# Inverse root of the norm: ScalarE's square root, VectorE's reciprocal and a Newton step in place of GpSimd's power

## The chip, the cores and the metric

The kernel runs on one core of one Trainium2 chip. The metric is the device time of one execution in microseconds (us). Five runs of the kernel before gave a median of 1666.22 us, from 1665.01 to 1666.94. Engines are called by the names of the profile: PE (TensorE's matmul), PEld (its weight load), DVE (VectorE), ACT (ScalarE), POOL (GpSimd) and SP (SyncE, which issues DMAs).

## The reference

An attention without softmax, whose output rows are normed per head, feeds a mixture of four experts that are all computed and weighted. Everything is float32.

```python
# q, k, v: (8, 8, 576, 64)
kv = np.einsum('bhsd,bhse->bhde', k, v)
out = np.einsum('bhsd,bhde->bhse', q, kv)
rms = np.sqrt(np.mean(out * out, axis=-1, keepdims=True) + 1e-06)
x = out / rms * g_norm          # then (B,H,S,D) -> (4608, 512)
p = domain_probs / (domain_probs.sum(-1, keepdims=True) + 1e-09)
for e in range(4):              # w1: (4, 512, 1024), w2: (4, 1024, 512)
    h = np.maximum(x @ w1[e], 0.0)
    out += p[:, e:e + 1] * (h @ w2[e])
```

The change concerns the factor 1 / rms: one number for each row and head, 64 elements wide.

## The kernel before, in words

**Work and stages.** The 4608 rows of x are cut into 9 chunks of 512 rows: the first 512 rows of each of 8 batches, and one chunk of the 64 rows that each batch leaves over. The outer loops go over experts and, inside, over chunks (lines 1671 to 1708), so there are 36 steps. A step multiplies by w1 (`up`, or `up_plain` for the first), applies the relu, multiplies by w2 (`down` or `down_deep`), and sends the weighted result to memory. The products are made in fewer multiplications by a two-level scheme of sums and differences of blocks (Strassen's kind). PE does the products (line 410), and DVE, POOL and ACT make the sums (line 433), copy banks of PSUM away (line 1262 and 1576) and merge results (lines 1406 and 1413). Weights and stored forms of x are loaded by SP.

**Attention in between.** The first expert's steps carry the attention of the next batch with them. `opening` does batch 0 ahead of everything, one pair of heads at a time; `attention` does batches 1 to 7, each in two parts of four heads. A part is: k by v (line 1001), a copy of the result (line 1013), q by that (`attend`, lines 1028 and 1037, into two "ab" and two "db" banks), copies of these banks to SBUF (lines 909 and 910, on DVE or ACT), squares (line 927, ACT, back into ab banks), sums over 64 elements (line 933, DVE), the inverse root, the scaling (line 950, DVE), a transposition on PE (`turn_x`, line 1069) and copies with the gain (line 1078, ACT). The left-over rows of both parts are normed together and transposed at line 1090. The opening has the same chain at lines 742 to 814: square 640, sum 647, power 654 and 658, scaling 667, transposition 806, copy 814.

**The norm.** `scaled` (opening, 5 calls) and `norm_rows` (attention, 21 calls) have a function `power` that issues two POOL instructions: a scaling of the sum of squares `ss` by 1/D with the constant added (lines 654 and 940), and ALU power with exponent -0.5 out of the constant tile `mhalf` into `rt` (lines 658 and 944). `ss` and `rt` have two buffers each.

**What sets the order.** Nothing is issued in the order in which it stands in the source. Each piece of work is given to `plan.add` with a key (its place in the steps), a cost for each engine that may do it, and what it reads and writes. `Plan.layout` then plays the program through in planned time: an engine that is free takes, among the operations within reach of its first open key, one whose inputs and buffers are ready, PE and SP the first one, the others the most urgent. Operations with two costs go to whichever of DVE and POOL takes them first. Buffers are assigned on the way. The result is a fixed order of instructions for each engine; on the chip every engine works through its own in that order and waits at each instruction for what it needs. So a changed cost can change every order after it. The costs are measured-looking constants, for instance

```python
def pe(products, columns, passes=2):
    return {"PE": passes * products * (0.0025 + columns / 1200.0) + 0.003}
```

and the constants 1.42 for `key_values` (line 1008) and 1.45 for `attend` (line 1043). `port=True` marks operations that DVE and POOL are kept from doing at the same time. While the first attention's data arrive, the planner fills PE's gaps with transpositions of the identity (line 1712).

Of the kernel before, what the change touches and what calls it, by code (L numbers as in the profile page):

```python
# [10 lines left out]
ACT = mybir.ActivationFunctionType  # L11
ALU = mybir.AluOpType
AX = mybir.AxisListType
ENG = mybir.EngineType
F32 = mybir.dt.float32
# [280 lines left out]
def kernel(  # L296
# [36 lines left out]
    nc = tc.nc  # L333

    B, H, S, D = q.shape
    E, DM, F = moe_w1.shape
    P = nc.NUM_PARTITIONS
# [15 lines left out]
    dram = ctx.enter_context(tc.tile_pool(name="dram", bufs=1, space=bass.MemoryType.DRAM))  # L353

    ident = const.tile([P, P], F32, name="ident")
    mhalf = const.tile([P, 2 * H], F32, name="mhalf")
    gcol = const.tile([P, 1], F32, name="gcol")
    p_all = const.tile([P, NBLK, E], F32, name="p_all")
    tot = const.tile([P, NBLK], F32, name="tot")
# [2 lines left out]
    BANKS = {"u1": 2, "u2": 2, "db": 2, "ab": 2}  # L362
    SHAPE = {
        "big": (31, 2 * NT), "w1y": (7, 768), "xf": (5, 2 * NT), "snap": (5, HN),
        "ss": (2, 2 * H), "rt": (2, 2 * H),
    }
    slots = {
        kind: [
# [32 lines left out]
    plan = Plan()  # L401

    def pe(products, columns, passes=2):
        return {"PE": passes * products * (0.0025 + columns / 1200.0) + 0.003}

    def halves_of(out_, lhsT, rhs, **kw):

# [212 lines left out]
    def x_halves(c):  # L620
        if c not in halves:
            halves[c] = [Buf("big", f"x{c}_{dh}") for dh in range(2)]
        return halves[c]

    def scaled(key, name, raw, n, x, blocks):

        width = blocks * D
        ss, rt = Buf("ss", f"ss{name}"), Buf("rt", f"rt{name}")

        def src(r):
            return raw[r].ap[0:n, 0:width].rearrange("p (b d) -> p b d", d=D)

        for r in range(2):
            plan.add(
                key, act(width),
                lambda eng, r=r: nc.scalar.activation(  # L640
                    out=x.ap[0:n, r * width:(r + 1) * width], in_=raw[r].ap[0:n, 0:width],
                    func=ACT.Square),
                reads=[raw[r]], parts=[x],
            )
        plan.add(
            key, dve(2 * width),
            lambda eng: nc.vector.reduce_sum(
                out=ss.ap[0:n, 0:2 * blocks],
                in_=x.ap[0:n, 0:2 * width].rearrange("p (b d) -> p b d", d=D), axis=AX.X),
            reads=[x], writes=[ss],  # L650
        )

        def power(eng):
            nc.gpsimd.tensor_scalar(
                out=ss.ap[0:n, 0:2 * blocks], in0=ss.ap[0:n, 0:2 * blocks], scalar1=1.0 / D,
                scalar2=EPS, op0=ALU.mult, op1=ALU.add,
            )
            nc.gpsimd.tensor_tensor(
                out=rt.ap[0:n, 0:2 * blocks], in0=ss.ap[0:n, 0:2 * blocks],
                in1=mhalf[0:n, 0:2 * blocks], op=ALU.pow,  # L660
            )

        plan.add(key - 0.3, {"POOL": 0.3 + 0.37 * blocks}, power, reads=[ss], writes=[ss, rt])
        for r in range(2):
            plan.add(
                key, dve(width),
                lambda eng, r=r: nc.vector.tensor_tensor(
                    out=x.ap[0:n, 0:2 * width].rearrange("p (b r d) -> p b r d", r=2, d=D)[:, :, r, :],
                    in0=src(r),
                    in1=rt.ap[0:n, r * blocks:(r + 1) * blocks].unsqueeze(2).to_broadcast(  # L670
                        [n, blocks, D]),
                    op=ALU.mult,
                ),
                reads=[raw[r], rt], **{"parts" if r else "writes": [x]},
            )
# [212 lines left out]
    def attention(b, key, span, rem):  # L888
# [25 lines left out]
        def norm_rows(key, name, x, squares, count):  # L914

            ss, rt = Buf("ss", f"ss{name}"), Buf("rt", f"rt{name}")
            width = count * D

            def by_head(ap):
                return ap.rearrange("p (b d) -> p b d", d=D)  # L920

            for at_ in range(0, width, NT):
                n = min(width, NT)
                sq = squares or Buf("ab", f"sq{name}_{at_}")
                plan.add(
                    key, act(n),
                    lambda eng, sq=sq, at_=at_, n=n: nc.scalar.activation(
                        out=sq.ap[:, 0:n], in_=x.ap[:, at_:at_ + n], func=ACT.Square),
                    reads=[x], writes=[sq],
                )  # L930
                plan.add(
                    key, dve(n),
                    lambda eng, sq=sq, at_=at_, n=n: nc.vector.reduce_sum(
                        out=ss.ap[:, at_ // D:(at_ + n) // D], in_=by_head(sq.ap[:, 0:n]),
                        axis=AX.X),
                    reads=[sq], parts=[ss],
                )

            def power(eng):
                nc.gpsimd.tensor_scalar(  # L940
                    out=ss.ap[:, 0:count], in0=ss.ap[:, 0:count], scalar1=1.0 / D, scalar2=EPS,
                    op0=ALU.mult, op1=ALU.add,
                )
                nc.gpsimd.tensor_tensor(  # L944
                    out=rt.ap[:, 0:count], in0=ss.ap[:, 0:count], in1=mhalf[:, 0:count], op=ALU.pow)

            plan.add(key - 0.3, {"POOL": 0.3 + 0.19 * count}, power, reads=[ss], writes=[ss, rt])
            plan.add(
                key, dve(width),
                lambda eng: nc.vector.tensor_tensor(  # L950
                    out=by_head(x.ap[:, 0:width]), in0=by_head(x.ap[:, 0:width]),
                    in1=rt.ap[:, 0:count].unsqueeze(2).to_broadcast([P, count, D]), op=ALU.mult,
                ),
                reads=[x, rt], writes=[x], port=True,
            )

        xr, xs = Buf("snap", f"x{b}_r"), Buf("snap", f"xs{b}")
        for s in range(2):
# [37 lines left out]
            def key_values(eng, bank=kbank, held=held):  # L996
# [8 lines left out]
                            )  # L1005

            plan.add(
                when, {"PE": 1.42}, key_values, reads=[t for ts in held for t in ts],
                writes=[kbank],
            )  # L1010
            plan.add(
# [9 lines left out]
            def attend(eng, raw=raw, rest=rest, kv=kv, qt=qt, s=s):  # L1021
# [18 lines left out]
                        )  # L1040

            plan.add(
                at(2 * s + 1.0), {"PE": 1.45}, attend, reads=[qt, kv], writes=raw + rest,
                early=True, gang=True,
            )
            when = at(2 * s + 1.4)
# [668 lines left out]

    with tc.manual_schedule(engines={ENG.PE, ENG.DVE, ENG.Activation, ENG.Pool, ENG.SP}):
        make_identity(nc, ident[:])
        nc.vector.memset(mhalf[:], -0.5)
        held = None
        wide = {}  # L1720
        for op in order:
            if op.seed:
                bank, n = op.marks
                assert wide.get((bank.kind, bank.slot), 0) >= n, "a seed would be overwritten"
            elif op.eng == "PE":
                for b in op.outs:
                    wide[b.kind, b.slot] = op.marks[1] if op.marks else 0
            made = op.fn(op.eng)
            if op.port and op.eng == "DVE":
                held = made.ins.name  # L1730
            elif op.port and op.eng == "POOL" and held is not None:
                tc.add_manual_dep(made.ins, held, mybir.DependencyInfo(
                    mybir.DependencyClass.Sync, mybir.DependencyReason.DATA
                ), reason="SBUF port")
# [28 lines left out]
```

## Time and profile before

| | before |
|---|---|
| median of 5 runs | 1666.22 us (1665.01 to 1666.94) |
| the profiled execution's own time | 1666.88 us |
| its span, first to last instruction | 1664.9 us |
| mean granted clock of PE | 0.999 |
| busy: PE, DVE, ACT, POOL | 1652.3, 1249.1, 971.0, 704.6 us |
| chain that ended last: PE's share | 97% |
| power of 16, 8, 4 columns (lines 944, 658) | 3206, 1647, 1140 ns |

The profile is of one execution. Times in it count from the span's start. A group of instructions shows how often it ran, its total, the mean of one, and how long its engine stood idle just before it, with what ended that idle time ("releaser"). PE's busy time holds everything between a matmul's start and its modelled end, so also the time that it takes longer at a lower clock. "PEclk" is the share of full clock that PE was granted. A timeline gives start and duration of merged runs of like instructions, and in brackets the idle time ahead of them.

### The profile page before, as it was taken

What the parts mean: (1) busy time and instruction counts of PE and PEld (TensorE: products, weight loads), DVE (VectorE), ACT (ScalarE), POOL (GpSimd) and SP (SyncE); (2) the same over time, 40 slices, a digit from 0 to 9 for tenths busy, and PEclk for the clock granted to TensorE, in tenths of its full rate; (3) what the DMA queues carried; (4) which work ended last, traced back from release to release, by engine and by line L of the source; (5) the groups of instructions that cost most, each with busy time, mean ns of one, the idle gap of its engine ahead of it and who ended that gap; (6) DMA issues with size and microseconds to landing.
All of it is one profiled execution on the core that took longest, in us unless ns stands there. A gap on an engine that the chain in (4) does not pass through costs nothing.

```text
span 1664.9 us, 66253 instructions
## 1 busy us (share of the span) xinstructions
PE 1652.3 (99%) x28884; PEld 1557.9 (94%) x28884; DVE 1249.1 (75%) x2051; ACT 971.0 (58%) x2391; POOL 704.6 (42%) x701
## 2 busy tenths in 40 slices
PE   9999999999999999999999999999999999999998
PEld 6587888888899999999999999999999999999996
DVE  4768777677788877777778777777788778777774
ACT  3355555554456666666666665656666566666662
POOL 2545453343445343433354554333355455333321
PEclk9999999999999999999999999999999999999999
DMA  9876765535466454444577444444578444444443
GB/s 218 194 228 185 217 176 145 144 126 182 147 168 150 125 122 116 110 114 113 139 182 178 116 117 115 107 113 116 132 178 202 116 116 116 104 115 116 116 104 52
DMA packets 208123, 234.27 MB, mean 141 GB/s; under 512 B 97368, under 2 KB 148440, under 8 KB 207832
## 3 DMA queue, kind: packets, MB, share of 16 engines
q1 hardware_dynamic: 184760, 193.32, 38.6%
q0 software_dynamic: 23072, 36.71, 15.2%
q8 instruction: 227, 3.72, 0.9%
q14 instruction: 64, 0.52, 0.1%
HBM read 155.79 MB, written 74.19 MB: 138 GB/s over the span
## 4 chain that ended last, share of the span: by engine, by line
PE 97%; DVE 1%; DMA 1%; POOL 0%; SPq 0%; issue 0%; ACT 0%; DVEq 0%; POOLq 0%; ACTq 0%
PE u L410 47%; PE db L410 32%; PE ab L410 15%; PE ab L1001 1%; PE ab L1069 1%; PE ab L1028 1%; DMA big<-in_q_dram 0%; DMA big<-in_moe_w_dram 0%; DVE big L433 0%; SPq L439 0%; POOL rt L944 0%; PE ab L1712 0%; PE ab L1090 0%; PE db L1037 0%; DVE small L950 0%
## 5 line engine op out<-in xcount | busy, mean ns | idle before, releaser
L433 DVE TENSOR_TENSOR big<-big,big 128x1024 f32<-128x1024 f32 (+1 forms) x527 | 518.6, 1001 | 39.6 <-ACT big L1226 15.9
L410 PE MATMUL u<-xf,big 128*64 128x128 f32 x6784 | 486.9, 273 | 0.2
L410 PEld LDWEIGHTS u<-xf,big 128*64 128x64 f32 x6784 | 394.0, 137 | 5.4 <-issue 1.0
L410 PE MATMUL u<-xf,w1y 128*64 128x128 f32 x5304 | 385.8, 273 | 0.0
L410 PE MATMUL db<-big,big 128*64 128x128 f32 (+1 forms) x4280 | 361.2, 308 | 2.1 <-DVE snap L909 1.1
L1270 DVE TENSOR_TENSOR big<-u,snap 128x256 f32<-128x256 f32 x476 | 199.5, 421 | 209.3 <-PE u L410 136.3
L433 POOL TENSOR_TENSOR big<-big,big 128x256 f32<-128x256 f32 (+1 forms) x196 | 218.9, 1134 | 226.0 <-DVE big L433 116.7
L410 PEld LDWEIGHTS u<-xf,w1y 128*64 128x64 f32 x5304 | 308.9, 137 | 2.4 <-issue 1.0
L410 PEld LDWEIGHTS db<-big,big 128*64 128x64 f32 x4280 | 262.3, 137 | 43.6 <-issue 2.8
L1262 ACT ACTIVATE snap<-u 128x256 f32<-128x256 f32 x490 | 187.5, 383 | 195.7 <-PE u L410 142.5
L1262 ACT ACTIVATE big<-u 128x256 f32<-128x256 f32 x476 | 181.0, 383 | 66.6 <-PE u L410 41.4
L1576 ACT ACTIVATE snap<-db 128x256 f32<-128x256 f32 (+1 forms) x230 | 82.0, 357 | 116.9 <-PE db L410 106.6
L1226 ACT ACTIVATE big<-big 128x1024 f32<-128x1024 f32 x134 | 140.7, 1050 | 5.6 <-DVE big L433 3.7
L433 POOL TENSOR_TENSOR big<-big 128x512 f32<-128x512 f32 (+1 forms) x76 | 94.3, 1247 | 114.9 <-DVE big L433 82.1
L410 PE MATMUL db<-small,big 128*64 128x128 f32 (+1 forms) x1552 | 116.9, 274 | 0.0
L1429 POOL DMA_DIRECT2D out_dram<-big x108 | 94.3, 1003 | 50.2 <-ACT big L1406 48.0
L1584 DVE TENSOR_TENSOR big<-ab,snap 128x256 f32<-128x256 f32 x166 | 69.9, 421 | 56.2 <-ACT snap L1576 30.1
L1262 ACT ACTIVATE u<-u 128x256 f32<-128x256 f32 x245 | 91.2, 372 | 24.8 <-PE u L410 9.1
L433 DVE TENSOR_TENSOR big<-big 128x512 f32<-128x512 f32 (+1 forms) x131 | 101.0, 783 | 1.0 <-PE u L410 1.0
L1614 POOL TENSOR_TENSOR big<-big 128x512 f32<-128x512 f32 x21 | 26.7, 1274 | 173.6 <-DVE big L433 140.9
L1406 ACT ACTIVATE big<-big,p_all 128x256 f32<-128x256 f32 x200 | 94.5, 501 | 5.4 <-POOL big L1614 4.0
L410 PEld LDWEIGHTS db<-small,big 128*64 128x64 f32 x1552 | 91.3, 137 | 0.7
(193 smaller groups left out, 2336.6 us busy)
## 6 DMA issues: line engine op xcount, KB each, us to landing
xf<-x SPq DMA_DIRECT2D x108, 512.0 KB, 3.6
out_dram<-big POOLq DMA_DIRECT2D x92, 256.0 KB, 5.5
xf<-x_h SPq DMA_DIRECT2D x81, 256.0 KB, 3.3
xf<-x SPq DMA_DIRECT2D x81, 256.0 KB, 3.6
x<-xf SPq DMA_DIRECT2D x36, 512.0 KB, 4.2
big<-in_moe_w_dram SPq DMA_DIRECT2D x32, 512.0 KB, 5.0
x_h<-big SPq DMA_DIRECT2D x18, 512.0 KB, 3.6
out_dram<-big SPq DMA_DIRECT2D x32, 256.0 KB, 3.7
```

The lines of the kernel that those rows point to most:

```text
L410: nc.tensor.matmul(out_[cols], lhsT=lhsT[:, cols], rhs=rhs, **kw)
L433: lambda eng: adder(eng).tensor_tensor(out=out_(), in0=a(), in1=b(), op=op),
L1001: nc.tensor.matmul(bank.ap[r * D:(r + 1) * D, o * D:(o + 1) * D], lhsT=ks[r], rhs=vs[r], start=(j == 0), stop=(j == len(sets) - 1), skip_g ...
L1028: nc.tensor.matmul(raw[r].ap[c * D:(c + 1) * D, (o * NR + t) * D:(o * NR + t + 1) * D], lhsT=qt.ap[half, col:col + D], rhs=kv.ap[half, o * ...
L1226: lambda eng: nc.scalar.activation(out=b.ap[:], in_=b.ap[:], func=ACT.Relu),
L1262: lambda eng: nc.scalar.activation(out=where(), in_=ps.ap[:, 0:HN], func=ACT.Copy),
L1270: lambda eng: nc.vector.tensor_tensor(out=block(whole, a, t), in0=src.ap[:, 0:HN], in1=add_.ap[:], op=ALU.add),
L1406: lambda eng: nc.scalar.activation(out=cell(i, half), in_=ap(), func=ACT.Copy, scale=prob()),
L1429: nc.gpsimd.dma_start(out=dst, in_=cell(i)[parts, :], accum_op=ALU.add)
L1576: lambda eng: nc.scalar.activation(out=where(), in_=group_of(ps.ap), func=ACT.Copy),
L1584: lambda eng: nc.vector.tensor_tensor(out=cell(tq, dq), in0=group_of(src.ap), in1=group_of(add_.ap), op=ALU.add,),
L1614: lambda eng: adder(eng).tensor_tensor(out=whole(to), in0=whole(a), in1=whole(b), op=ALU.add),
```

## The change

The function `power` goes in both places, and with it the tile `mhalf`. A new function `inverse_root` adds two operations to the plan: `root` on ACT, which writes sqrt(ss/D + eps) into `rt`, and `invert` on DVE, four instructions: the reciprocal of `rt` in place, and one Newton step for the inverse root in three instructions that multiply with a scalar and a tensor, with a second part of `rt` (now twice as wide) as scratch. `eps` is a column of constants for ACT's bias. Three costs of the planner change as well: each PE product loses its 3 ns, `key_values` goes from 1.42 to 1.2, and `attend` of batches 1 to 7 from 1.45 to 1.33. Other planner rules are untouched.

```diff
--- before.py
+++ after.py
@@ -353,7 +353,7 @@
     dram = ctx.enter_context(tc.tile_pool(name="dram", bufs=1, space=bass.MemoryType.DRAM))
 
     ident = const.tile([P, P], F32, name="ident")
-    mhalf = const.tile([P, 2 * H], F32, name="mhalf")
+    eps = const.tile([P, 1], F32, name="eps")
     gcol = const.tile([P, 1], F32, name="gcol")
     p_all = const.tile([P, NBLK, E], F32, name="p_all")
     tot = const.tile([P, NBLK], F32, name="tot")
@@ -362,7 +362,7 @@
     BANKS = {"u1": 2, "u2": 2, "db": 2, "ab": 2}
     SHAPE = {
         "big": (31, 2 * NT), "w1y": (7, 768), "xf": (5, 2 * NT), "snap": (5, HN),
-        "ss": (2, 2 * H), "rt": (2, 2 * H),
+        "ss": (2, 2 * H), "rt": (2, 4 * H),
     }
     slots = {
         kind: [
@@ -401,7 +401,7 @@
     plan = Plan()
 
     def pe(products, columns, passes=2):
-        return {"PE": passes * products * (0.0025 + columns / 1200.0) + 0.003}
+        return {"PE": passes * products * (0.0025 + columns / 1200.0)}
 
     def halves_of(out_, lhsT, rhs, **kw):
 
@@ -622,6 +622,27 @@
             halves[c] = [Buf("big", f"x{c}_{dh}") for dh in range(2)]
         return halves[c]
 
+    def inverse_root(key, ss, rt, n, count):
+
+        def root(eng):
+            nc.scalar.activation(
+                out=rt.ap[0:n, 0:count], in_=ss.ap[0:n, 0:count], func=ACT.Sqrt, scale=1.0 / D,
+                bias=eps[0:n, :],
+            )
+
+        def invert(eng):
+            a, r, w = ss.ap[0:n, 0:count], rt.ap[0:n, 0:count], rt.ap[0:n, 2 * H:2 * H + count]
+            nc.vector.reciprocal(out=r, in_=r)
+            nc.vector.scalar_tensor_tensor(
+                out=w, in0=a, scalar=D * EPS, in1=r, op0=ALU.add, op1=ALU.mult)
+            nc.vector.scalar_tensor_tensor(
+                out=w, in0=w, scalar=-0.5 / D, in1=r, op0=ALU.mult, op1=ALU.mult)
+            return nc.vector.scalar_tensor_tensor(
+                out=r, in0=w, scalar=1.5, in1=r, op0=ALU.add, op1=ALU.mult)
+
+        plan.add(key - 0.3, {"ACT": 0.2}, root, reads=[ss], writes=[rt])
+        plan.add(key - 0.3, {"DVE": 0.75}, invert, reads=[ss, rt], writes=[ss, rt], port=True)
+
     def scaled(key, name, raw, n, x, blocks):
 
 
@@ -650,17 +671,7 @@
             reads=[x], writes=[ss],
         )
 
-        def power(eng):
-            nc.gpsimd.tensor_scalar(
-                out=ss.ap[0:n, 0:2 * blocks], in0=ss.ap[0:n, 0:2 * blocks], scalar1=1.0 / D,
-                scalar2=EPS, op0=ALU.mult, op1=ALU.add,
-            )
-            nc.gpsimd.tensor_tensor(
-                out=rt.ap[0:n, 0:2 * blocks], in0=ss.ap[0:n, 0:2 * blocks],
-                in1=mhalf[0:n, 0:2 * blocks], op=ALU.pow,
-            )
-
-        plan.add(key - 0.3, {"POOL": 0.3 + 0.37 * blocks}, power, reads=[ss], writes=[ss, rt])
+        inverse_root(key, ss, rt, n, 2 * blocks)
         for r in range(2):
             plan.add(
                 key, dve(width),
@@ -936,15 +947,7 @@
                     reads=[sq], parts=[ss],
                 )
 
-            def power(eng):
-                nc.gpsimd.tensor_scalar(
-                    out=ss.ap[:, 0:count], in0=ss.ap[:, 0:count], scalar1=1.0 / D, scalar2=EPS,
-                    op0=ALU.mult, op1=ALU.add,
-                )
-                nc.gpsimd.tensor_tensor(
-                    out=rt.ap[:, 0:count], in0=ss.ap[:, 0:count], in1=mhalf[:, 0:count], op=ALU.pow)
-
-            plan.add(key - 0.3, {"POOL": 0.3 + 0.19 * count}, power, reads=[ss], writes=[ss, rt])
+            inverse_root(key, ss, rt, P, count)
             plan.add(
                 key, dve(width),
                 lambda eng: nc.vector.tensor_tensor(
@@ -1005,7 +1008,7 @@
                             )
 
             plan.add(
-                when, {"PE": 1.42}, key_values, reads=[t for ts in held for t in ts],
+                when, {"PE": 1.2}, key_values, reads=[t for ts in held for t in ts],
                 writes=[kbank],
             )
             plan.add(
@@ -1040,7 +1043,7 @@
                         )
 
             plan.add(
-                at(2 * s + 1.0), {"PE": 1.45}, attend, reads=[qt, kv], writes=raw + rest,
+                at(2 * s + 1.0), {"PE": 1.33}, attend, reads=[qt, kv], writes=raw + rest,
                 early=True, gang=True,
             )
             when = at(2 * s + 1.4)
@@ -1715,7 +1718,7 @@
 
     with tc.manual_schedule(engines={ENG.PE, ENG.DVE, ENG.Activation, ENG.Pool, ENG.SP}):
         make_identity(nc, ident[:])
-        nc.vector.memset(mhalf[:], -0.5)
+        nc.vector.memset(eps[:], EPS)
         held = None
         wide = {}
         for op in order:
```

## The prediction

> **What bounds the kernel now.** I read the page first (busy shares, chain), then the waits of PE, then the stretch in which PE waits, by timeline and by windows.
>
> ```profile
> span 1664.9 us, 66253 instructions
> ...
> PE 1652.3 (99%) x28884; PEld 1557.9 (94%) x28884; DVE 1249.1 (75%) x2051; ACT 971.0 (58%) x2391; POOL 704.6 (42%) x701
> ...
> PE 97%; DVE 1%; DMA 1%; POOL 0%; SPq 0%; issue 0%; ACT 0%; DVEq 0%; POOLq 0%; ACTq 0%
> ```
>
> PE is busy for all but 12.6 us. Taking 71 us of work off POOL can't by itself move the end; only a change in what PE waits for can. These are the waits (total, times, longest, us):
>
> ```profile
> PE ab L1069 <- DVE ss L933: 2.5, 1, 2.5
> PE ab L1712 <- POOL ident masks.py:199: 1.4, 1, 1.4
> PE db L410 <- DVE snap L909: 1.1, 1, 1.1
> PE ab L1069 <- DVE small L950: 0.8, 1, 0.8
> ```
>
> The second is the start. The others lie behind a norm. The timeline (start, duration) has the chain of the first two:
>
> ```profile
> 55.78 2.36 POOL L433 TENSOR_TENSOR big<-big,big 128x1024 f32<-128x1024 f32 x1 [10.29 <-DMA big<-in_moe_w_dram]
> ...
> 58.22 1.06 POOL L940 TENSOR_SCALAR ss<-ss 128x16 f32<-128x16 f32 x1
> ...
> 59.37 3.75 POOL L944 TENSOR_TENSOR rt<-ss,mhalf 128x16 f32<-128x16 f32 x1
> ...
> 60.73 1.95 PE L410 MATMUL db<-big,big 128*64 128x256 f32 x16 [1.07 <-DVE snap L909]
> ...
> 63.15 1.23 DVE L950 TENSOR_TENSOR small<-small,rt 128x1024 f32<-128x1024 f32 x1 [1.01 <-POOL rt L944]
> ...
> 65.16 1.25 PE L1069 MATMUL ab<-ident,small 128*128 128x128 f32 x8 [2.48 <-DVE ss L933]
> ```
>
> The sums were reduced by 53.4, but the power queues behind a POOL add that waited for weights, and ends at 63.12; the scaling and a reduction follow, and PE starts at 65.16. The next view shows what that costs afterwards (PEclk is the figure ahead of the DMA share):
>
> ```profile
> 62.60:65.20 2.60, 0.12 (x3) 0.05 (x1) 2.02 (x3) 0.47 (x1) 1.20 (x2) 1.00 0.79 175
> 65.20:66.60 1.40, 1.40 (x10) 0.99 (x12) 1.40 (x3) 0.75 (x2) 1.40 (x1) 1.00 0.00 0
> 66.60:70.00 3.40, 3.40 (x20) 1.88 (x18) 3.40 (x6) 0.54 (x1) 3.23 (x3) 0.51 0.69 112
> ```
>
> After the hole PE runs 3.4 us at half clock: 1.7 us more, hidden in "busy".
>
> [...] Here the load took 1283 ns,[...] and a pointer scale adds 90 ns (687 against 597 at 128x512). [...] reciprocal[...] here 378 ns against 182 for a scalar add on the same 36 elements. [...] L940 took 1.06 us beside a DVE add, usually 0.2.
>
> **The change, part by part.** There are 26 norms: 5 in the opening (8 columns), 14 of 16 columns, 7 of 4.
>
> *Removed.* 52 POOL instructions: by form 44.9+8.0+4.3+4.5+6.6+1.7+0.8+0.2 = 71 us. None is on the path except through the waits above.
>
> ```profile
> L944 POOL TENSOR_TENSOR rt<-ss,mhalf 128x16 f32<-128x16 f32 x14 | 44.9, 3206 | 1.2
> L466 DVE RECIPROCAL inv<-tot 128x36 f32<-128x36 f32 x1 | 0.4, 378 | 0.0
> L465 DVE TENSOR_SCALAR tot<-tot 128x36 f32<-128x36 f32 x1 | 0.2, 182 | 0.0
> ```
>
> *Added on ACT.* 26 Sqrt. Between 0.22 (the 128x64 copy, L774)[...]; I take 0.29, 7.5 us. One table load: the built order has just one more, ahead of the first Sqrt, none later. It falls at 11.7 us, after a copy, where ACT idled 1.0 us. Cost 1.3 (trace)[...]. Queued behind it are Sqrt and the qT copy of pair 2, whose readers on PE come at 16.4, so I take nothing; if that cover failed, up to 1.5 us.
>
> *Added on DVE.* 104 small instructions. Reciprocal of 16: 0.145 (intercept of 0.28 at 128 and 0.42 at 256 columns) plus 16 x 5.4 ns (378-182 over 36) = 0.24; each of the three others 0.16. Sum 0.72 a norm, 19 us in all; bounds 0.29 (four of the 72-ns memset) and 1.2 (0.378 + 3 x 0.28). DVE would be 76% busy.
>
> *Latency.* Reduction to scaling: before 0.30+3.21 and three hops of 0.1 = 3.8 us; after 0.29+0.72 and hops = 1.3, without POOL's queue.
>
> *Moved.* Costs in the planner change too (each product 3 ns less, key_values 1.42 to 1.2, attend 1.45 to 1.33), and it orders everything anew; the five engines' orders differ nearly throughout. PE's instructions are the same in number and shape: 12552+784+64 products, 62 fillers. SP's issues keep their order up to the first x stores (about 54 us). On DVE and POOL five 1024-wide adds have changed places with five 128-wide ones.
>
> **The sum**, by walking the new order with the durations above.
> Opening to 36.6 us: the fillers move from before the first up product to after the last transposition; the 0.38 us wait at 21.96 goes. -0.4 (-0.8 to +1.5).
> 52 to 70 us: before 1.07+2.48+0.23+1.7 = 5.5, plus 0.3 by which L1001 is stretched at 53.12 (1.63 against 1.34). In the new order one more up product stands ahead of the second attend. DVE takes the w2 add first, which must wait for weights at 55.8, so the second reduction ends at 57.7 and the attend waits 0.8. The first down product needs a db bank emptied by ACT at 60.3: wait 1.15. The second needs the one that DVE empties after add, four small steps and scaling, at 62.5: wait 0.4. The first turn then finds all ready; the second waits 0.7 for its scaling. Total 3.05, in pieces:[...] no half clock. -2.75 (-5 to +1).
> 127.52: its wait of 0.82 was behind the power. Between the end of attend and its turn the order gives 9.7 us of PE work, and the chain needs some 6. -0.8.
> About 150: the two attends of batch 3 are 3.5 us of PE work apart (5.0 before); evacuation, squares and two reductions with a 1.23 us add between them take 4.2. +0.7 (0 to 2).
> All else: later turns have 8 to 14 us of cover. Waits at 1634 to 1636 (0.76) stem from the last seeds, with no norm near: 0. For new waits I can't see, +0.5 (0 to 4).
> Sum -0.4-2.75-0.8+0.7+0.5 = -2.75: 1664.1 against the profiled execution's 1666.88. That one lies 0.66 above the median, so 1663.5 against 1666.22, 0.17% less. A measurement of this kernel tells some 0.2% (3.3 us) from no change.
>
> **The rivals.**
> *The wait moves[...].* The 3.05 us of waits fall close together; if weights come 1 us later,[...] 1.7 us return: 1665.2. For: two of the four waits hang on DMA or on DVE's queue. Against: each is short. 0.20.
> *Slower: Sqrt blocks ACT.* In ACT's queue Sqrt waits for DVE's reduction, and the copies that empty PE's u banks stand behind it; POOL had nothing PE needed so soon. If the reduction is late by more than about 0.9 us (two products of 0.44), PE stops. At 0.4 us for each of 21 attention norms: 8.4, so 1663.0+8.4 = 1671.4. For: DVE is 72 to 78% busy there and adds take 1.23. Against: ACT is only 56% busy and PE has four u banks. 0.17.
> *Nearly all waits go*: weights arrive in time and the bank empties early; the 3.05 fall to 1 and the 0.5 and 0.7 to nothing: 1660.3. 0.10.
> *The change doesn't do what it says*: a table load at each Sqrt would cost 52 x 1.3. The built order excludes it.
>
> **How the numbers follow.** Forecast 0.53, spread 1661 to 1666; nearly half of it lies below 1662.9 (-0.2%). Faster: 0.26+0.10 = 0.36. Slower: all but a little of 0.17 = 0.16. Same: 0.48. The range 1660.5 to 1669.5 leaves out some 0.05 below and 0.14 above.
>
> **What would show it.** Right: POOL near 635 to 640 us busy, DVE near 1265, ACT near 979; PE busy about 1.7 lower with no half clock after 60 us; Sqrt to scaling below 1.5 us. Wrong: PEclk below 0.9 between 60 and 75; PE waits on ACT L1265 or L1081 of over 3 us in all; steps above 0.3 us each; a wait beyond 430 us, which would be the new order and not the norm.

## The result, and the profile after

| | before | after |
|---|---|---|
| median of all runs | 1666.19 us (41 runs, 1663.98 to 1669.4) | 1663.04 us (23 runs, 1661.24 to 1665.13) |
| the profiled execution's own time, span | 1666.88, 1664.9 us | 1663.56, 1661.4 us |
| busy: PE, DVE, ACT, POOL | 1652.3, 1249.1, 971.0, 704.6 us | 1651.0, 1283.2, 976.9, 648.7 us |

The ratio is 0.9983, 95% interval 0.9977 to 0.9988: 0.17% faster. The forecast was 1663.5 us and the measurement is 0.5 us below it. That agreement says less than it seems to: the experiments show that the forecast's cause was only a part of what happened, and that errors in its terms offset each other.

The page of the changed kernel (span, busy times, chain of work that ended last):

```profile
span 1661.4 us, 66359 instructions
...
PE 1651.0 (99%) x28884; PEld 1557.8 (94%) x28884; DVE 1283.2 (77%) x2153; ACT 976.9 (59%) x2420; POOL 648.7 (39%) x649
...
PE 99%; ACT 0%; issue 0%; DVE 0%; POOL 0%; POOLq 0%; ACTq 0%; DVEq 0%
```

PE's share of the chain rose from 97 to 99%. What PE still waits for, in the changed kernel (total, times, longest):

```profile
PE ab L772 <- issue: 2.0, 1, 2.0
PE db L410 <- ACT snap L921: 1.4, 1, 1.4
PE ab L1715 <- POOL ident masks.py:199: 1.4, 1, 1.4
PE db L410 <- ACT snap L1579: 0.4, 1, 0.4
```

No wait behind a norm is left in this execution. The first line is the opening's data, which came later here than in the profile of before (0.46 us there), so that PE reaches the stretch below later too. The timeline of the changed kernel where the hole was (start, duration):

```profile
58.94 0.30 ACT L628 ACTIVATE rt<-ss,eps 128x16 f32<-128x16 f32 x1
59.27 0.25 DVE L635 RECIPROCAL rt<-rt 128x16 f32<-128x16 f32 x1
...
59.97 0.17 DVE L640 SCALAR_TENSOR_TENSOR rt<-rt 128x16 f32<-128x16 f32 x1
...
62.04 1.22 DVE L953 TENSOR_TENSOR small<-small,rt 128x1024 f32<-128x1024 f32 x1
...
63.18 3.67 PE L410 MATMUL db<-big,big 128*64 128x256 f32 x32 [1.42 <-ACT snap L921]
...
66.78 1.09 PE L1072 MATMUL ab<-ident,small 128*128 128x128 f32 x8
```

From the start of the square root to the end of the last step is 1.2 us. The scaling nevertheless starts 1.9 us after that, because VectorE's queue has an addition in front of it that waits for a copy by ACT; but PE has 3.67 us of products ahead of the turn (66.78), which starts without a wait. The windows of the same stretch (PEclk is the figure ahead of the DMA share):

```profile
59.50:63.20 3.70, 2.28 (x80) 1.33 (x76) 2.85 (x6) 2.09 (x6) 0.00 (x0) 1.00 0.91 294
...
66.60:70.00 3.40, 3.40 (x36) 2.42 (x32) 3.19 (x13) 1.94 (x4) 0.00 (x0) 1.00 0.70 170
```

No half clock follows (1.00 in both windows).

To see where time is won and lost, each profile was read at fixed points of PE's order, the k-by-v products (line 1001) of a batch's part. There, *lost time* is the trace time minus the PE work that the order puts ahead of that point, with every product at the duration that it has in undisturbed stretches of the traces, from start to start (0.109 us for 64x128, 0.219 for 64x256, 0.4375 for 64x512). The work is 1642.5 us in all. The last column is the span less the lost time by batch 7: the work, and what is lost after it. Lost time by then, in us (the filling of hole filled is counted as lost):

| profile of | batch 1 | batch 2 | batch 3 | batch 7, second part | span minus that |
|---|---|---|---|---|---|
| before | 6.04 | 13.55 | 15.55 | 18.80 | 1646.1 |
| before, second profile | 5.99 | 12.28 | 14.28 | 17.52 | 1646.1 |
| after | 8.59 | 11.28 | 11.94 | 15.81 | 1645.6 |
| order kept | 7.06 | 11.79 | 18.52 | 23.33 | 1646.1 |
| steps late | 7.32 | 14.70 | 19.84 | 23.49 | 1646.5 |
| hole filled | 8.62 | 12.61 | 14.59 | 18.28 | 1646.1 |
| short power | 8.78 | 11.22 | 13.20 | 16.42 | 1646.1 |
| one norm | 5.88 | 10.98 | 12.97 | 16.28 | 1646.1 |
| old norm, new costs | 7.79 | 10.32 | 11.46 | 14.96 | 1646.8 |
| old norm, product cost | 6.35 | 12.82 | 14.82 | 17.69 | 1646.9 |
| new norm, old costs | 7.47 | 10.56 | 12.95 | 15.46 | 1649.3 |
| power in new order | 8.70 | 12.70 | 13.65 | 21.16 | 1645.5 |
| Newton twice | 6.52 | 11.11 | 11.76 | 16.03 | 1645.6 |
| no Newton | 9.21 | 11.90 | 12.55 | 16.48 | 1645.6 |

The first column is chance: with one and the same order of PE it runs from 5.88 to 8.78, as the first data land (hole filled, whose opening is that of before to the last instruction, has 8.62). By batch 2 most of that has gone again: the three profiles of the changed kernel's order with ScalarE's square root, 6.52 to 9.21 at batch 1, are 11.11 to 11.90 there. Between stands the addition that waits for weights, and what follows it is tied to the time at which they land: a PE that comes there late waits less. So the second column, not the depth of the hole, tells what a change gains up to there, and a difference of 0.8 in it can still be chance.

Before to after: 2.3 us by batch 2, 1.3 more by batch 3, 0.6 back by batch 7, and 0.5 at the end: 3.5 us, the difference of the spans.

### The profile page after: what moved, and what is told of

Same layout as the page of the kernel before. It is cut to its first block, busy times and chain, and to the rows that moved or that the text cites. A ratio compares the mean times of both kernels' runs of the same rounds, so it can differ in the third digit from the quotient of the medians.

```text
span 1661.4 us, 66359 instructions
## 1 busy us (share of the span) xinstructions
PE 1651.0 (99%) x28884; PEld 1557.8 (94%) x28884; DVE 1283.2 (77%) x2153; ACT 976.9 (59%) x2420; POOL 648.7 (39%) x649
## 4 chain that ended last, share of the span: by engine, by line
PE 99%; ACT 0%; issue 0%; DVE 0%; POOL 0%; POOLq 0%; ACTq 0%; DVEq 0%
PE u L410 48%; PE db L410 32%; PE ab L410 15%; PE ab L1004 1%; PE ab L1031 1%; PE ab L1072 1%; PE ab L1715 1%; PE ab L772 0%; PE db L1040 0%; PE ab L753 0%; PE ab L1093 0%; PE ab L817 0%; DVE ss L944 0%; ACT L628 0%; PE db L799 0%
## 5 line engine op out<-in xcount | busy, mean ns | idle before, releaser
L433 DVE TENSOR_TENSOR big<-big,big 128x1024 f32<-128x1024 f32 (+1 forms) x518 | 503.0, 984 | 40.6 <-ACT big L1229 17.5
L410 PE MATMUL u<-xf,big 128*64 128x128 f32 x7072 | 507.6, 273 | 0.2
L410 PEld LDWEIGHTS u<-xf,big 128*64 128x64 f32 x7072 | 410.4, 137 | 5.6 <-issue 1.7
L1273 DVE TENSOR_TENSOR big<-u,snap 128x256 f32<-128x256 f32 x458 | 191.8, 420 | 175.3 <-PE u L410 138.1
L433 POOL TENSOR_TENSOR big<-big,big 128x256 f32<-128x256 f32 (+1 forms) x166 | 198.8, 1201 | 158.8 <-DVE big L433 93.4
L433 DVE TENSOR_TENSOR big<-big 128x512 f32<-128x512 f32 (+1 forms) x128 | 111.3, 877 | 0.0
L1617 POOL TENSOR_TENSOR big<-big 128x512 f32<-128x512 f32 x28 | 35.7, 1276 | 184.3 <-DVE big L433 168.5
L410 PE MATMUL db<-small,big 128*64 128x128 f32 x1416 | 106.4, 273 | 0.4 <-ACT snap L1579 0.4
L410 PE MATMUL ab<-big,big 128*64 128x128 f32 (+1 forms) x1344 | 93.6, 278 | 0.0
L410 PE MATMUL db<-kv,big 128*64 128x128 f32 x1264 | 87.4, 273 | 0.0
```

Source lines behind the costliest of these rows:

```text
L410: nc.tensor.matmul(out_[cols], lhsT=lhsT[:, cols], rhs=rhs, **kw)
L433: lambda eng: adder(eng).tensor_tensor(out=out_(), in0=a(), in1=b(), op=op),
L1273: lambda eng: nc.vector.tensor_tensor(out=block(whole, a, t), in0=src.ap[:, 0:HN], in1=add_.ap[:], op=ALU.add),
L1617: lambda eng: adder(eng).tensor_tensor(out=whole(to), in0=whole(a), in1=whole(b), op=ALU.add),
```

## The experiments

Two theories stood at the start of the experiments. *Latency*: the gain comes from the norm's shorter latency, as forecast. *Order*: the planner, fed with other costs, laid a better order, and the norm has little to do with it. A third came from the first run, *queue*: the new norm's steps cost time in VectorE's queue. Every ratio is to runs of the kernel before made beside it on the same chip (medians 1666.0, 1666.3 and 1666.34 us).

**Order kept.** The new norm, issued where the power stood in the old order.

```diff
             def power(eng):
-                nc.gpsimd.tensor_scalar(
-                ...
-                    out=rt.ap[:, 0:count], in0=ss.ap[:, 0:count], in1=mhalf[:, 0:count], op=ALU.pow)
+                inverse_root(ss, rt, P, count)
             plan.add(key - 0.3, {"POOL": 0.3 + 0.19 * count}, power, reads=[ss], writes=[ss, rt])
```

> The norm changed alone: ACT's square root and the four DVE instructions are issued at the place where the two POOL instructions stood, and the planner still believes in POOL and in its old costs, so PE and SP keep the order of before. Theory N (the norm's latency made the gain): the scaling at 63.15 comes about 1 us earlier, the turn at 65.16 too, the half clock after it and the wait of 0.8 at 127.5 go: about 1666.2 - 1.0 - 1.7 - 0.8 = 1662.7. Theory O (the new order made the gain, the norm only gave the planner other numbers): no gain, 1666.2, or up to 1668 because a queue stands behind a square root that the plan never placed.

Measured: 1669.93 us, ratio 1.0026 (1.0015 to 1.0036). Slower. The hole at 60 us shrank, but between batch 2 and batch 3 PE lost 6.7 us (11.79 to 18.52) where before it lost 2.0. The timeline of that stretch, with the new norm in the old order:

```profile
121.17 0.32 ACT L627 ACTIVATE rt<-ss,eps 128x16 f32<-128x16 f32 x1
121.52 0.25 DVE L628 RECIPROCAL rt<-rt 128x16 f32<-128x16 f32 x1 [0.42 <-ACT rt L627]
...
125.39 0.16 DVE L628 RECIPROCAL rt<-rt 128x4 f32<-128x4 f32 x1
125.52 0.66 PE L410 MATMUL u<-big,w1y 128*64 128x128 f32 x8 [0.97 <-DVE big L1269]
...
126.39 1.21 DVE L949 TENSOR_TENSOR small<-small,rt 128x1024 f32<-128x1024 f32 x1
...
127.66 1.97 PE L1068 MATMUL ab<-ident,small 128*128 128x128 f32 x8 [1.48 <-DVE small L949]
```

And the window after it:

```profile
127.60:131.20 3.60, 3.54 (x16) 2.57 (x18) 3.60 (x5) 2.08 (x3) 2.35 (x1) 0.50 0.38 101
```

VectorE is busy for all but 0.1 us from 124 to 136 us; before, it was too. Eight new steps and their 0.42 us of waiting for the square root come on top, PE stands 0.97 and 1.48 us, and then it runs at half clock (0.50 for 3.60 us). The half clock is not the whole loss: the two of its eight runs with a mean clock of 1.000 took 1668.01 and 1669.38 us, against a median of 1664.97 for such runs of before. So the steps are not free in this order.

**New norm, old costs.** The planner knows the new norm; the three constants stay.

```diff
+        plan.add(key - 0.3, {"ACT": 0.2}, root, reads=[ss], writes=[rt])
+        plan.add(key - 0.3, {"DVE": 0.75}, invert, reads=[ss, rt], writes=[ss, rt], port=True)
```

> The new norm, known to the planner, with the three old costs (3 ns per product, 1.42, 1.45). Theory N: the gain stays, 1662 to 1664. Theory O in the form that the three costs made the order better: 1666 or so.

Measured: 1667.01 us, ratio 1.0006 (0.9998 to 1.0014). The attention is as good as in the changed kernel (15.46 against 15.81 by batch 7). It loses 3.7 us (1649.3 against 1645.6) after 345 us, where no norm runs: PE stands 1.4 us between 340 and 1600 us in eight places, mostly for copies and sums that empty its banks, and 0.76 us at the end instead of 0.38. That is not all of it, as the view counts a stop as idle time only from a product's modelled end, some 0.17 us after the next could have started (a matmul of 128 columns stands in it with 0.273 us, and the pairs that make a product follow each other at 0.109). Taken from one matmul's start to the next, everything longer than usual by 0.03 us or more adds up to 6.0 us after batch 7, and to 2.4 in the changed kernel: that is the 3.7.

**Old norm, new costs.** GpSimd's power, with two of the three constants new (`key_values` stays at 1.42).

```diff
-        return {"PE": passes * products * (0.0025 + columns / 1200.0) + 0.003}
+        return {"PE": passes * products * (0.0025 + columns / 1200.0)}
...
-                at(2 * s + 1.0), {"PE": 1.45}, attend, reads=[qt, kv], writes=raw + rest,
+                at(2 * s + 1.0), {"PE": 1.33}, attend, reads=[qt, kv], writes=raw + rest,
```

> POOL's power as before, with two of the three new costs (no 3 ns per product, attend 1.33; key_values stays at 1.42). Theory N: PE still waits behind the power, 1665 to 1668. Theory O: as fast as after, 1663.

Measured: 1663.0 us, ratio 0.9983 (0.9976 to 0.9991). As fast as the changed kernel, without the new norm. Its timeline shows why:

```profile
55.12 0.21 POOL L940 TENSOR_SCALAR ss<-ss 128x16 f32<-128x16 f32 x1 [7.89 <-DVE ss L933]
55.41 2.91 POOL L944 TENSOR_TENSOR rt<-ss,mhalf 128x16 f32<-128x16 f32 x1
...
56.27 1.23 DVE L433 TENSOR_TENSOR big<-big,big 128x1024 f32<-128x1024 f32 x1 [1.03 <-DMA big<-in_moe_w_dram]
```

In this order the addition that waits for weights is VectorE's. GpSimd has nothing ahead of the norm, and the power ends at 58.3 instead of 63.1 us. Its lost time is 3.2 us less than before by batch 2 and 3.8 by batch 7 (2.0 and 2.6 against the second profile).

**Hole filled.** The kernel before with 14 transpositions of the identity ahead of batch 1's first turn, so that PE doesn't stand.

```diff
+                for _ in range(fill):
+                    nc.tensor.transpose(slots["u1"][0][:, 0:P], ident[:], ident[:])
```

> Before, with 14 transpositions of the identity (about 1.8 us at full clock) put in front of the first turn of batch 1, into a bank that is free, so that PE is busy while it waits for the scaling. The turn itself can start no earlier. [...] the 3.4 us at half clock go and the time falls by 1.7 to 1664.5. If the half clock is only a figure of the record, or the waits behind it would have filled with the same time, it stays at 1666.2.

Measured: 1666.44 us, ratio 0.9999 (0.9991 to 1.0007): no difference. Two windows of its profile:

```profile
16.00:20.00 4.00, 2.94 (x50) 2.49 (x49) 0.42 (x1) 0.82 (x2) 1.19 (x1) 0.65 1.05 386
...
60.00:70.00 10.00, 10.00 (x90) 6.74 (x86) 8.74 (x13) 4.95 (x11) 8.43 (x4) 1.00 0.85 176
```

PE was busy and at full clock from 60 to 70 us, but the filling only stands where PE would have stood (1.75 us), and the turn starts when it did before, at 65.18 us. This execution has its half clock at 17 us instead (0.65 from 16 to 20 us), in the opening, where the first data came late (PE waits 1.66 us up to 17.06). So the profile doesn't show what the half clock behind the hole is worth. The runs with a mean clock of 1.000 show no gain either: 1666.08 us in the median of seven, against 1664.97 for 18 such runs of before.

**Short power.** A multiplication of the same shape in place of the power; the inverse root is left out, and only the time counts.

```diff
-                    out=rt.ap[:, 0:count], in0=ss.ap[:, 0:count], in1=mhalf[:, 0:count], op=ALU.pow)
+                    out=rt.ap[:, 0:count], in0=ss.ap[:, 0:count], in1=mhalf[:, 0:count], op=ALU.mult)
```

> The kernel before, with the power (lines 658, 944) replaced by a multiplication of the same shape on GpSimd: the inverse root is left out, so the norm's factor is a different number. Every engine's order is that of before, and VectorE and ScalarE get no new work. It isolates the latency of the power. Latency theory (the forecast's): the hole at 60 to 65 us and its half clock go (-2.8, as the run with the order kept gained by 74 us) and the 0.82 us wait at 127 goes (-0.8): 1662.4 us, nothing lost later. Order theory (the old order is worse by itself, whatever the norm costs): 1665 us or more. Queue theory (the new norm's steps in VectorE's queue are what cost 4.7 us at 120 to 134 us with the order kept): agrees with 1662.4 here.

Measured: 1664.35 us, ratio 0.9986 (0.998 to 0.9993). The latency alone is worth some 2 us of the expected 3.6. In lost time it is 1.1 against the second profile of before, all of it by batch 2. The wait at 127 us stayed (0.80, at 125.17 here):

```profile
120.57 0.22 POOL L944 TENSOR_TENSOR rt<-ss,mhalf 128x16 f32<-128x16 f32 x1
...
123.91 1.21 DVE L950 TENSOR_TENSOR small<-small,rt 128x1024 f32<-128x1024 f32 x1
...
125.17 1.09 PE L1069 MATMUL ab<-ident,small 128*128 128x128 f32 x8 [0.80 <-DVE small L950]
```

The factor is ready 3.1 us before the scaling starts: there the scaling is held up by VectorE's queue and not by the power. Order kept is 5.6 us slower than this (5.9 when each is set against the runs of before beside it): that is what the steps on VectorE and ACT cost in the old order, with the half clock that follows and some 0.7 us of longer latency a norm (1.2 against 0.5).

**Power in the new order.** The changed kernel's order, with GpSimd's two instructions at the square root's place and nothing in place of the steps.

```diff
         def root(eng):
-            nc.scalar.activation(...)
+            nc.gpsimd.tensor_scalar(
+                out=a, in0=a, scalar1=1.0 / D, scalar2=EPS, op0=ALU.mult, op1=ALU.add)
+            nc.gpsimd.tensor_tensor(out=r, in0=a, in1=mhalf[0:n, 0:count], op=ALU.pow)
```

> The changed kernel's order, but at the place of each square root GpSimd does its old scaling and power, and the four VectorE steps are left out. Order theory: the new order has the cover that the norm needs, so 1663 us give or take 1, although the power takes 3.2 us again. Latency theory: the norm is late again by 2.5 us wherever the next turn is close; a hole of over 2 us with half clock comes back between 58 and 75 us, and the time is 1665.5 us or more. GpSimd near 715 us busy, VectorE near 1264 in both.

Measured: 1673.47 us (five runs, 1668.5 to 1673.97), ratio 1.0043 (1.0029 to 1.0057). The slowest of all, and 10.4 us above the changed kernel: the order theory expected 1663. The profile is of the best of the five runs. Three of the others have mean clocks of 0.997 and 0.998, but the slowest has 0.999, so half clock alone is not the reason. Its timeline around 70 us:

```profile
67.31 2.90 POOL L631 TENSOR_TENSOR rt<-ss,mhalf 128x16 f32<-128x16 f32 x1
...
70.25 1.23 DVE L946 TENSOR_TENSOR small<-small,rt 128x1024 f32<-128x1024 f32 x1 [3.08 <-POOL rt L631]
71.53 1.09 PE L1065 MATMUL ab<-ident,small 128*128 128x128 f32 x8 [1.26 <-DVE small L946]
```

VectorE stands 3.08 us behind the power, then PE 1.26. So this order relies on the fast norm.

**Steps late.** As order kept, with the four steps issued right ahead of the scaling.

```diff
+            def scale(eng):
+                invert(ss, rt, P, count)
+                return nc.vector.tensor_tensor(
```

> As with the order kept, but the reciprocal and the Newton steps are issued right ahead of the scaling that reads them, not at the power's old place; so the additions that empty PE's u banks stand ahead of them in VectorE's queue. The work is the same. With the order kept, PE lost 4.7 us at 120 to 134 us (2.45 us of waits, then half clock). Queue theory (steps in VectorE's queue ahead of bank-emptying additions are the loss): the waits on line 1269 go, the loss falls to 1.5 us or less, 1666.5 us. If the square root in ScalarE's queue or the sum of VectorE's work is the cause: 1669 us or more again.

Measured: 1669.54 us, ratio 1.002 (1.0011 to 1.003). No better than order kept; 1666.5 was expected. PE waits 1.71 us for the scaling at 129.55 and 0.77 for the merge of line 1413 (1420 in this kernel) at 131.41, again with half clock after (0.87 and 0.70 in the four us from 128 and from 132). Behind the reduction at the hole it waits 2.3 us again. Moving the steps within VectorE's queue didn't help: queued or moved, the work stands ahead of something that PE needs, because VectorE has no gap there. One thing is open: the only one of its nine runs with a mean clock of 1.000 took 1666.6 us, so without the half clock the moved steps may cost less than order kept's.

**Newton twice.** The changed kernel's order with a second Newton step.

```diff
-            nc.vector.scalar_tensor_tensor(
+            for _ in range(2):
+                nc.vector.scalar_tensor_tensor(
```

> The changed kernel with a second Newton step: three more VectorE instructions per norm (78 in all, some 0.17 us each, 13 us of VectorE work), the order of everything else as in the changed kernel. If VectorE has slack at every norm in the new order: 1663.0 us within 0.7. Queue theory (a VectorE that is saturated between 118 and 135 us passes each added step on to PE): 1664 to 1667 us, with waits on VectorE near 120 to 135 us and perhaps a stretch at half clock there.

Measured: 1663.8 us, ratio 0.9987 (0.998 to 0.9993); 0.76 us above the changed kernel for 78 more instructions, 10 ns each. The intervals of the two ratios overlap. Batch 2 to 3 loses as little as in the changed kernel (0.65 against 0.66). Before batch 2 there is a wait that the changed kernel's profile doesn't have:

```profile
69.95 1.09 PE L1074 MATMUL ab<-ident,small 128*128 128x128 f32 x8 [1.75 <-DVE small L955]
```

Ahead of this scaling stand the second steps of two norms (16 and 4 columns), 1.2 us, and PE had come to batch 1 2.1 us earlier than in the changed kernel's profile. Some 0.5 us of the wait would stay with one step; that is an estimate from these two figures, and no profile of the changed kernel with early data shows it.

**One norm.** The kernel before, with only the first norm of batch 1 exchanged.

```diff
+                if name == "1_0":
+                    inverse_root(ss, rt, P, count)
+                    return
```

> The kernel before with one single norm exchanged, the first of batch 1 (the one that queues behind the addition that waits for weights, in front of the hole at 60 us); the 25 others keep the power. Every order is that of before. Latency theory: this norm alone makes the hole, so PE gains 2.8 us or more by 74 us, as with all norms exchanged, and since VectorE gets four steps only, nothing is lost at 120 to 134 us: 1663.4 us. Order theory: 1665.5 us or more.

Measured: 1665.46 us, ratio 0.9994 (0.9986 to 1.0002). About 0.9 us of the 2.8 expected, and not clear of no change. Its timeline:

```profile
57.63 0.17 DVE L635 SCALAR_TENSOR_TENSOR rt<-ss,rt 128x16 f32<-128x16 f32 x1
57.72 1.22 DVE L434 TENSOR_TENSOR big<-big,big 128x1024 f32<-128x1024 f32 x1
...
60.64 1.22 DVE L966 TENSOR_TENSOR small<-small,rt 128x1024 f32<-128x1024 f32 x1
61.90 1.29 DVE L946 TENSOR_REDUCE ss<-ab 128x8 f32<-128x512 f32 x2
...
62.64 1.25 PE L1085 MATMUL ab<-ident,small 128*128 128x128 f32 x8 [1.37 <-DVE ss L946]
```

The factor is ready at 57.8 us. The old order has two wide additions and two copies ahead of the scaling on VectorE, which starts at 60.64; PE then waits for the reduction behind it, which frees its ab bank. Removing the power brings the next thing in VectorE's queue to light, 1.1 us earlier (1.37 against 2.48).

**Old norm, product cost.** One constant alone, the 3 ns.

```diff
-        return {"PE": passes * products * (0.0025 + columns / 1200.0) + 0.003}
+        return {"PE": passes * products * (0.0025 + columns / 1200.0)}
```

> The kernel before with one planner constant changed, the 3 ns of each PE product; norm, attend (1.45) and key_values (1.42) as before. PE's order is the old one up to about 120 us, hole included, and new from there on. If the planner's constant is what made the old norm with new costs as fast as the changed kernel: 1663 us. If it was that that order puts the norm of batch 1 clear of the addition that waits: this one keeps the hole and gives 1666.2 us, within 1.5.

Measured: 1666.52 us, ratio 1.0 (0.9991 to 1.0008). The hole is there again (2.5 us behind line 933). By batch 7 it has lost 17.69 us where old norm, new costs has lost 14.96, which is nearly the whole difference of the two spans. So the smaller cost isn't a gain by itself. That the gain comes with an order that gives the waiting addition to VectorE fits both orders, but these are two cases that differ elsewhere too.

**No Newton.** The changed kernel without the Newton step.

```diff
             nc.vector.reciprocal(out=r, in_=r)
-            nc.vector.scalar_tensor_tensor(
-            ...
-                out=r, in0=w, scalar=1.5, in1=r, op0=ALU.add, op1=ALU.mult)
```

> The changed kernel without the Newton step: the reciprocal of the square root is used as it is; every other instruction in the changed kernel's order. VectorE loses 78 instructions (13 us of work). Queue theory: twice the Newton step cost 0.8 us more than the changed kernel, so without it 0.3 to 1 us less, 1662.4 us. If VectorE's steps lie beside other work in this order: 1663.0 us within 0.4.

Measured: 1662.69 us, ratio 0.9979 (0.997 to 0.9989). The lowest median of all, 0.35 us below the changed kernel, with overlapping intervals. With the 0.76 of the second step, a Newton step in all 26 norms costs between 0.3 and 0.8 us, if it costs anything: in this order nearly all of VectorE's new work lies beside other work.

**Before again.** A second profile of the kernel before.

> The kernel before, a second profile. The order is fixed, so the waits behind the power at 60 to 66 us should be there again with over 3 us in all, and the half clock after them; what differs is when the first data arrive (the first attention's wait was 0.46 us in the profile of before and 2.0 in the changed kernel's).

Measured: 1665.7 us (one run), span 1663.6. The hole is the same (2.5 us behind line 933 at 63.94), the clock is not:

```profile
60.60:64.00 3.40, 0.92 (x9) 0.35 (x6) 2.36 (x4) 0.54 (x2) 2.00 (x2) 1.00 0.73 194
64.00:67.40 3.40, 3.07 (x24) 1.84 (x25) 3.40 (x6) 1.29 (x2) 3.23 (x3) 1.00 0.39 63
```

PE was busy for 27% of 3.4 us and kept its full clock. So the half clock belongs to executions and not to the kernel (0.83 from 64 to 68 us in the first profile, 1.00 in the second); by batch 2 the two profiles are 1.3 us apart. Of 115 runs of before that list their mean clock (beside the experiments), 47 have 1.000 (median 1665.32 us), 43 have 0.999 (1666.93) and 25 have 0.998 (1666.63). Of the changed kernel's 23 runs, 14 have 1.000 (1662.47) and 9 have 0.999 (1664.09). At 1.000 the difference is 2.85 us.

The 1.6 us between 1.000 and 0.999 are not the price of the hole, because a mean clock doesn't say where the clock was halved. In the profiles of short power, hole filled, power in new order and no Newton it was at 17 us, in the opening: 16 transposing products took 1.60 to 1.98 us there, and 1.09 in before. Only in before and in old norm, product cost was it behind the hole (0.83 and 0.72 from 64 to 68 us). And one norm's runs at 0.999 (four, 1665.02) are no slower than those at 1.000 (nine, 1665.46).

## Why the prediction was right, and where it was not

**Opening (-0.4).** Not told by the profiles: the arrival of the first data moves this by up to 2.9 us between executions of one order, more than the term. The wait at 17 us, 2.0 instead of 0.46, is such a case.

**52 to 70 us (-2.75).** Up to batch 2 the two profiles differ by 2.3 us with the opening, against 3.15 forecast for both. The mechanism was half right. The power behind the waiting addition did hold PE (short power gains 2 us), but the prediction took 5.5 us of hole and half clock as the price of that one norm. Two parts of this were mis-sized. The half clock behind the hole comes in some executions and is not a constant of the order (one of the two profiles of before has it). That waits in pieces leave the clock at full was an estimate of the author's; in this execution they did, at 1.00 with a wait of 1.42 us. And after the power the old order has VectorE's additions, which keep 1.37 of the 2.48 us (one norm). Of the four new waits forecast (0.8, 1.15, 0.4, 0.7), only that for the db bank came, at 1.42. The others don't show: 3.05 forecast, 1.4 measured. In part that is luck of this execution, whose first data came late: in Newton twice, the same order with earlier data, PE waits 1.42, 0.2 and 1.75 us, and 1.2 of the last are the added steps. Whether the rival of a second half clock came true in some runs is open: 9 of 23 have a mean clock of 0.999, but in the two profiles of this order with half clock (no Newton, power in new order) it lies at 17 us.

**127 us (-0.8) and later (+0.7, +0.5).** The stretch to batch 3 gained 1.3. The forecast gave the wait to the power; short power shows that it was VectorE's queue (0.80 left), so the new order took it away. From batch 3 to 7 the changed kernel loses 0.6 more than before, forecast 1.2. In it are 0.43 for the second attend of batch 3 (1.59 instead of 1.16), which was the forecast's +0.7.

**End (0).** It gained 0.5, of which 0.38 is one of the two waits after 1630 us. No norm is near: that is the order.

**The sum** came out near because its errors offset, which is luck. Against the profiles it has 0.85 too much gain by batch 2, 0.5 too little by batch 3, 0.6 too much loss from there to batch 7 and nothing for the end, where 0.5 was gained: 2.75 forecast, 3.5 measured between the two spans.

**Costs.** Square root 0.30 (26 of them, 0.283 to 0.319; the author's estimate was 0.29), reciprocal of 16 columns 0.24 (0.24), the other three 0.175 (0.16), the one added table load 1283 ns and hidden (PE waits for nothing of ACT's in the first 25 us). VectorE's 1283.2 us were forecast as 1265, GpSimd's 648.7 as 635 to 640: the new order gives them other shares of the additions, which was not priced.

**The step that failed** is in "Moved" and the sum: the planner's new order was walked for waits, while the gain was credited to the norm's latency. Latency alone gives 2 us in the old order. The new norm whole in the old order costs 3.9. A new order with the old norm gives 3.0 of the 3.2. And the new order with the old power costs 10.4 more. So the gain belongs to neither part: it belongs to an order that is laid for its own norm. That this order has to keep batch 1's norm clear of the addition that waits for weights is likely, from old norm, new costs against old norm, product cost; it was not tested alone. Nor is it enough: new norm, old costs has lost as little by batch 7 and gives its gain away after the attention. The rival *Sqrt blocks ACT* had the right side for the old order, but mostly the wrong engine: VectorE was the one without room, though with the order kept it stood 6.4 us in all behind square roots of 16 columns.

**Open**: half of the 10.4 us of the power in the new order, whose profile is of its best run.

## What to carry to other kernels

Where a planner lays the order, a changed operation comes with a new order, and the two have to be tested apart: the new operation in the old order, the old operation in a new order, and the old operation in the new one. A latency on the path is worth only the distance to the next thing in the queue (with one norm 1.1 of the 2.48 us); look what stands between it and the engine that waits before you count the whole wait. Small steps cost what the receiving engine's fullest stretch says and not what its mean load says: 104 steps, nearly all of 0.16 to 0.25 us, cost 5.6 to 5.9 us in the old order (with the square roots and the half clock), and in the new one an added or removed step moved the time by 5 to 10 ns, if at all.

## What the runs showed of the hardware

The same 2.5 us hole was followed by half clock in one profile of before and not in the other, although in the second a stretch of 3.4 us was 27% busy. In before the granted clock was 0.50 from 66.65 to 70.06 us, 3.41 us, and 1.00 in the 3.42 us ahead of that, of which PE was busy for 1.50 (44%). In order kept the share of 0.72 over the 12 us from 124 makes some 6.7 us of half clock. In the opening a wait of 1.66 us, up to 17.06, came ahead of half clock in hole filled (0.93 over the first 23.1 us), and one of 1.75 us, up to 16.79, ahead of full clock in new norm, old costs (1.00). So no limit can be read from these busy shares and waits, and what sets the half clock is not shown.

GpSimd's scaling of 16 columns (line 940) takes 0.20 us alone, and 1.06 at 58.22 us in before, where a 1024-wide VectorE addition is running when it starts; that of 4 columns took 1.23 at 71.35, beside a 1024-wide scaling. The power takes 3.75 us instead of 2.90 where such an addition is running, for instance at 59.37 us in before, where the addition ends at 60.35: the 0.85 us more are about what the addition had left, 0.98. An addition that starts while the power runs lengthens neither: in old norm, new costs the power from 55.41 us took 2.91 and the addition inside it, from 56.27, its usual 1.23.

The table load of 1283 ns (at 12.05 us in the changed kernel) was followed by the square root 0.02 us later.
